# Sums of x on another engine, even token groups and a last expert by eight products, in a fused attention and expert kernel

## The chip, the cores and the metric

The kernel runs on one core of a Trainium2 chip. The metric is the device time of one execution in microseconds; lower is better. A core has TensorE (matrix products, PE in the profile; its weight loads are PEld), VectorE (DVE), ScalarE (ACT), GpSimd (POOL) and SyncE (SP), which issues DMA transfers. Each engine takes its instructions in order and waits for semaphores of the others.

## The reference

Attention with a sketch of degree two gives x; then eight experts are applied to every token, weighted by a routing matrix P.

```python
# attention: B = H = 4, S = 1088, D = 32, r = 8
phi(x) = (S1 x)_i (S2 x)_j                       # 64 features
num = phi(q) @ (phi(k)^T v);  den = phi(q) . sum(phi(k)) + 1e-6
x = (num / den), as (B*S, H*D) = (4352, 128)
# routing: N, D, E, F = 4352, 128, 8, 1024
P = exp(x @ w_gate - max)
for _ in range(8):                               # rows, then columns, are normed
    P /= P.sum(1, keepdims=True) + 1e-9
    P /= P.sum(0, keepdims=True) + 1e-9
    P *= N / E
for e in range(E):
    out += P[:, e:e + 1] * (np.maximum(x @ w1[e], 0) @ w2[e])
```

All is float32.

## The kernel before, in words

**Two ways through an expert.** P is positive, so P * relu(x w1) w2 equals relu((P x) w1) w2. While attention and routing still run, TensorE fills its gaps with experts whose P is not known yet: the *unweighted* stage (`groups`) takes expert 0 for all tokens and expert 1 for tokens 0 to 1279, and keeps the results, transposed, in `kept[0]` and `kept[1]`. They are multiplied by P later, on GpSimd (L933, L935). All other pairs of token and expert are done in the *weighted* stage, the function `weighted()`, after routing.

**Token groups.** An entry of `groups` or `wgroups` is (first token, n, experts); it covers two halves of n tokens each. In the weighted stage `witems` lists (group, expert) pairs, 60 of them; odd groups take their experts in reverse, so that a group often begins with the expert with which the one before ended, whose weights then need no load (`same`). Groups are counted from 0 and so are items. Each item is done in two passes s = 0 and s = 1, for two halves of the hidden dimension; a pass of the first layer (`firsts`) and the second layer's products of the pass before it (`seconds`) are issued in turn, step by step.

**Seven products for eight.** Two blocks by two blocks are multiplied with seven block products and sums of blocks in the manner of Strassen and Winograd. That needs sums of the blocks of w1 (`sum_first`, L864 to L867, into `w1x`), of w2 (`sum_second`, L876 to L879, into `ws`), of x (`sum_x`: part 0 at L902 on GpSimd, parts 1 and 2 at L904 and L906 on VectorE, into `xf`) and of the hidden layer (VectorE, L1058 to L1066, into `ts`, beside the additions L977 and the relus L980). Item 0 uses eight products in the first layer, and group 0 eight in the second. Sums of weights are made once, in group 0, and written to DRAM (L870, L880); later groups load them (L845, L856).

**Where a product's inputs come from.** `weigh(i)` multiplies x by a row of P on GpSimd (L894, into `xf`) and swaps partition halves with two DMAs (L897). `aside`, called once per pass at its third step, puts GpSimd's work there: `weigh` of the item after next and the sums of the next item's weights, each after a one-column copy on ScalarE (`gate`, L989) that holds it back to this point. `spare(0)` and `spare(1)` are places for VectorE at the last two steps of a pass.

**Order of the transfers.** SyncE issues nearly all transfers of this stage in program order: for an item, raw or summed w1 of the next (L850 or L845), the row of P (L886), rows for the kept results (L931), the swaps (L897), the store of w1's sums (L870), w2 of the next (L854), and the store of ws's sums (L880) or their load (L856). A store waits for the sums it writes, and everything behind it waits too.

**End of a group.** Second-layer products accumulate in four PSUM banks `acc[g][rho][q]`. `ended(g, q)` copies them to the tile `z`, of which there is one (L1132, ScalarE). `finish_seven` lists the sums that make the output rows of it: two over z, then a swap of partition halves by DMA into `w` (L1155), nine more sums of 64 rows, and for each half an addition of the kept row (all at L1136), a transpose (L1183) and four stores, one for each head (L676); a store is cut in two at a batch boundary. The list `leisure` is worked off one entry at a time: two in `spare` at s = 0 (VectorE), one in `aside` if it is small and no chore for the kept rows is waiting (GpSimd). What is left at the end is worked off on VectorE.

In the weighted stage all engines keep the program's order (`manual_schedule`). A tile with one buffer may be written for its next use only after the last reader of its former use.

```python
def product(out, form, x, start, stop):
    for r in range(2):
        rows = slice(H2 * r, H2 * (r + 1))
        for col in range(2):
            o = P * s + H2 * col
            nc.tensor.matmul(out[H2 * col:H2 * (col + 1), r], w1[rows, form, o:o + H2], xf[rows, x], ...)
```

Of the kernel before, what the change touches and what calls it, by code (L numbers as in the profile page):

```python
# [10 lines left out]
F32 = mybir.dt.float32  # L11
# [39 lines left out]
def kernel(  # L51
# [477 lines left out]
    def routing():  # L529
# [45 lines left out]
        for b in (1, 0, 2, 3):  # L575
# [20 lines left out]
    kept = [keep.tile([P, N], F32, name="kept0"), keep.tile([P, 1280], F32, name="kept1")]  # L596
    items = [(g, e) for g, group in enumerate(groups) for e in group[2]]
# [301 lines left out]
    def sum_x(i, part_):  # L899
        xf = sources[i]  # L900
        if part_ == 0:
            nc.gpsimd.tensor_tensor(xf[:, 4:6], xf[:, 1:4:2], xf[:, 0:2], op=Alu.subtract)  # L902
# [19 lines left out]
    def chores_of(i):  # L922

        g, e = witems[i]
        lo, n, es = wgroups[g]
        o = [j for j, (h, _) in enumerate(witems) if h == g].index(i) - 1
        ys = [kept[x][:, lo:lo + 2 * n] for x in range(es[0])]
        if not 0 <= o < len(ys):
            return []
        pk = late[0].tile([P, 2 * NW], F32, tag="pk", name="pk", bufs=1)[:, 0:2 * n]  # L930
        nc.sync.dma_start(out=pk, in_=pT[o:o + 1, lo:lo + 2 * n].to_broadcast([P, 2 * n]))  # L931
        halves = [slice(n * t, n * (t + 1)) for t in range(2)]
        chores = [lambda c=c: nc.gpsimd.tensor_tensor(ys[o][:, c], ys[o][:, c], pk[:, c], op=Alu.mult) for c in halves]  # L933
        if o == 1:
            chores += [lambda c=c: nc.gpsimd.tensor_tensor(ys[0][:, c], ys[0][:, c], ys[1][:, c], op=Alu.add)  # L935
                       for c in halves]
        return chores


    def weighted():  # L940
# [16 lines left out]
        def firsts(t):  # L957
# [33 lines left out]
            def aside(y):  # L991


                now = i == 0 or g == 0 and s == 1
# [59 lines left out]
            add(h[:, 3], pc, p1)  # L1054
            if g == 0:
                relu(h[:, 3], h[:, 3])
# [5 lines left out]
            relu(flat(h[:, 1], n), pa)  # L1062
            if g:
                nc.vector.tensor_tensor(ts[:, 2], h[:, 1], ts[:, 0], op=Alu.subtract)  # L1064
# [5 lines left out]
        def seconds(t):  # L1070
# [74 lines left out]
        def finish_seven(g):  # L1145
# [27 lines left out]
            out_of(g, y)  # L1173

        def out_of(g, y):
            lo, n, es = wgroups[g]
            for t in range(2):
                at = lo + n * (1 - t)
                plus(y[:, t], y[:, t], kept[0][:, at:at + n])

                def put(engine, t=t, at=at):
                    yt = late[0].tile([P, NW // 32, 32], F32, tag="yt", name="yt", bufs=2)[:, 0:n // 32, :]
                    nc.vector.transpose(out=yt.rearrange("p b d -> p (b d)"), in_=y[:, t])  # L1183
                    store(yt, at // 32, (at + n) // 32)

                leisure.append((put, False))

# [123 lines left out]
```

## Time and profile before

| | |
|---|---|
| median of 3 runs | 957.92 us (957.33 to 958.08) |
| the profiled execution's own time | 956.46 us |
| its span, first to last instruction | 954.7 us |
| TensorE busy | 907.8 us (95%) |
| VectorE, ScalarE, GpSimd busy | 728.2, 556.8, 253.2 us |
| mean granted TensorE clock | 0.978 |
| read from and written to HBM | 139.33 MB, 19.57 MB |

Durations in the trace belong to the profiled execution. TensorE's products of different array quadrants run at the same time, so the records overlap, and busy is the time in which at least one runs. Idle time of an engine costs nothing unless the chain of waits passes through it. "Idle before" in brackets is the engine's wait ahead of an instruction and what ended it.

### The profile page before, as it was taken

What the parts mean: (1) busy time and instruction counts of PE and PEld (TensorE: products, weight loads), DVE (VectorE), ACT (ScalarE), POOL (GpSimd) and SP (SyncE); (2) the same over time, 40 slices, a digit from 0 to 9 for tenths busy, and PEclk for the clock granted to TensorE, in tenths of its full rate; (3) what the DMA queues carried; (4) which work ended last, traced back from release to release, by engine and by line L of the source; (5) the groups of instructions that cost most, each with busy time, mean ns of one, the idle gap of its engine ahead of it and who ended that gap; (6) DMA issues with size and microseconds to landing.
All of it is one profiled execution on the core that took longest, in us unless ns stands there. A gap on an engine that the chain in (4) does not pass through costs nothing.

```text
span 954.7 us, 35858 instructions
## 1 busy us (share of the span) xinstructions
PE 907.8 (95%) x15452; PEld 635.1 (67%) x15452; DVE 728.2 (76%) x1275; ACT 556.8 (58%) x1116; POOL 253.2 (27%) x298
## 2 busy tenths in 40 slices
PE   9999999988688999999999999999999999999992
PEld 5787544455455667767766776776677778788782
DVE  7688699722222688888888888888888889898894
ACT  3454555554345666666666666666666656666661
POOL 3121100163435222232213323322331232232220
PEclk9999999999879999999999999999999999999996
DMA  9994100456564777468658665856776695684951
GB/s 245 303 272 140 51 1 1 119 188 185 158 178 144 220 224 225 135 194 274 185 164 244 219 184 155 272 184 184 227 240 193 228 290 185 209 281 128 283 200 35
DMA packets 125918, 180.11 MB, mean 189 GB/s; under 512 B 28960, under 2 KB 93552, under 8 KB 118592
## 3 DMA queue, kind: packets, MB, share of 16 engines
q1 hardware_dynamic: 124016, 172.42, 58.9%
q0 software_dynamic: 1600, 5.36, 1.9%
q8 instruction: 122, 2.00, 0.9%
q14 instruction: 36, 0.29, 0.1%
q10 hardware_dynamic: 144, 0.03, 0.0%
HBM read 139.33 MB, written 19.57 MB: 166 GB/s over the span
## 4 chain that ended last, share of the span: by engine, by line
PE 59%; DVE 4%; ACT 2%; issue 2%; POOL 0%; DMA 0%; SPq 0%; ACTq 0%; DVEq 0%; POOLq 0%
PE pair L973 30%; PE s L1092 29%; DVE hb L977 1%; ACT z L1132 1%; DVE hb L1058 1%; DVE hb L1064 1%; DVE z L1136 1%; DVE hb L1065 0%; DVE hb L1066 0%; ACT copies L1036 0%; DMA w<-z 0%; POOL xf L902 0%; DVE y L1136 0%; ACT hb L980 0%; SPq L676 0%
## 5 line engine op out<-in xcount | busy, mean ns | idle before, releaser
L973 PE MATMUL pair<-xf,w1x 64*64 64x256 f32 (+2 forms) x6736 | 516.0, 371 | 27.5 <-POOL xf L902 20.1
L973 PEld LDWEIGHTS pair<-xf,w1x 64*64 64x64 f32 x6736 | 260.9, 134 | 132.9 <-POOL xf L902 23.5
L977 DVE TENSOR_TENSOR hb<-pair,copies 128x512 f32<-128x512 f32 (+2 forms) x354 | 234.1, 664 | 121.4 <-PE pair L973 60.1
L1092 PE MATMUL s<-hb,w 64*64 64x256 f32 (+2 forms) x3440 | 262.6, 374 | 0.2 <-ACT z L1132 0.2
L1092 PE MATMUL s<-hb,ws 64*64 64x256 f32 (+2 forms) x3392 | 255.6, 364 | 0.2 <-DVE hb L1065 0.2
L980 ACT ACTIVATE hb<-hb 128x512 f32<-128x512 f32 (+2 forms) x248 | 151.1, 611 | 119.2 <-DVE hb L977 116.9
L1092 PEld LDWEIGHTS s<-hb,w 64*64 64x64 f32 x3440 | 136.4, 136 | 50.8 <-issue 4.8
L1092 PEld LDWEIGHTS s<-hb,ws 64*64 64x64 f32 x3392 | 135.7, 133 | 42.6 <-DVE hb L1065 0.6
L894 POOL TENSOR_TENSOR xf<-xT,pb 128x512 f32<-128x512 f32 (+2 forms) x60 | 74.7, 1246 | 297.5 <-ACT xf L989 208.3
L902 POOL TENSOR_TENSOR xf<-xf 128x512 f32<-128x512 f32 (+2 forms) x59 | 74.7, 1266 | 192.9 <-ACT xf L989 171.2
L705 PE MATMUL a<-xT,w 128*64 128x416 f32 (+3 forms) x512 | 119.9, 462 | 0.0
L707 ACT ACTIVATE hb<-a 128x416 f32<-128x416 f32 (+3 forms) x128 | 59.3, 466 | 67.3 <-PE a L705 56.4
L1039 ACT COPY copies<-pair 128x512 f32<-128x512 f32 (+2 forms) x118 | 67.0, 568 | 52.8 <-PE pair L973 52.8
L980 ACT ACTIVATE hb<-pair 128x512 f32<-128x512 f32 (+2 forms) x126 | 72.5, 575 | 38.7 <-PE pair L973 38.7
L1042 ACT COPY copies<-pair 128x512 f32<-128x512 f32 (+2 forms) x118 | 66.7, 565 | 37.5 <-PE pair L973 37.5
L1036 ACT COPY copies<-pair 128x512 f32<-128x512 f32 (+2 forms) x118 | 67.0, 568 | 30.5 <-PE pair L973 30.5
L1058 DVE SCALAR_TENSOR_TENSOR hb<-hb 128x512 f32<-128x512 f32 (+2 forms) x106 | 72.2, 681 | 11.4 <-DVE hb L977 0.5
L1064 DVE TENSOR_TENSOR hb<-hb 128x512 f32<-128x512 f32 (+2 forms) x106 | 70.7, 667 | 2.2 <-ACT hb L980 1.1
L720 DVE TENSOR_TENSOR hb<-hb 128x416 f32<-128x416 f32 (+7 forms) x84 | 59.6, 709 | 16.7 <-ACT hb L707 13.4
L766 PE MATMUL s<-hb,ws 128*64 128x416 f32 (+3 forms) x224 | 69.8, 471 | 0.2 <-DVE hb L720 0.2
L1065 DVE SCALAR_TENSOR_TENSOR hb<-hb 128x512 f32<-128x512 f32 (+2 forms) x106 | 69.8, 658 | 0.0
L1066 DVE TENSOR_TENSOR hb<-hb 128x512 f32<-128x512 f32 (+2 forms) x106 | 69.8, 658 | 0.0
(165 smaller groups left out, 649.2 us busy)
## 6 DMA issues: line engine op xcount, KB each, us to landing
w1x<-w1x SPq DMA_DIRECT2D x53, 1024.0 KB, 5.2
w<-in_moe_w_dram SPq DMA_DIRECT2D x57, 512.0 KB, 5.0
ws<-ws SPq DMA_DIRECT2D x53, 512.0 KB, 5.9
pb<-pT SPq DMA_DIRECT2D x42, 256.0 KB, 5.2
xf<-xf SPq DMA_DIRECT2D x84, 128.0 KB, 2.6
w1x<-in_moe_w_dram SPq DMA_DIRECT2D x28, 128.0 KB, 3.9
ph<-qa SPq DMA_DIRECT2D x12, 288.0 KB, 4.7
rb<-qb SPq DMA_DIRECT2D x3, 1152.0 KB
```

Of the source, the lines that this page charges most:

```text
L705: nc.tensor.matmul(ph[sl], loaded_w[j][0][:, P * f + H2 * s:P * f + H2 * (s + 1)], xT[:, at + lo:at + hi], start=True, stop=True, tile_pos ...
L766: nc.tensor.matmul(sums[g][i][H2 * s:H2 * (s + 1)], w, x, start=c == 1, stop=c == per, tile_position=(0, H2 * s))
L894: nc.gpsimd.tensor_tensor(xf[:, 0:2].rearrange("p b n -> p (b n)"), xT[:, lo:lo + 2 * n], weights.pop(i), op=Alu.mult)
L902: nc.gpsimd.tensor_tensor(xf[:, 4:6], xf[:, 1:4:2], xf[:, 0:2], op=Alu.subtract)
L973: nc.tensor.matmul(out[H2 * col:H2 * (col + 1), r], w1[rows, form, o:o + H2], xf[rows, x], start=start, stop=stop, tile_position=(H2 * r, ...
L977: nc.vector.tensor_tensor(flat(out, n), x, flat(y, n), op=Alu.add)
L980: nc.scalar.activation(out=x, in_=y, func=Act.Relu)
L1058: nc.vector.scalar_tensor_tensor(ts[:, 0], h[:, 3], 0.0, h[:, 0], op0=Alu.max, op1=Alu.subtract)
L1064: nc.vector.tensor_tensor(ts[:, 2], h[:, 1], ts[:, 0], op=Alu.subtract)
L1065: nc.vector.scalar_tensor_tensor(ts[:, 1], h[:, 3], 0.0, h[:, 1], op0=Alu.max, op1=Alu.subtract)
L1066: nc.vector.tensor_tensor(ts[:, 3], h[:, 2], ts[:, 2], op=Alu.subtract)
L1092: yield lambda rho=rho, rows=rows, c=c: nc.tensor.matmul(acc[g][rho][q][H2 * half:H2 * (half + 1), n * place:n * (place + 1)], w[rows], fl ...
```

## The change

Three things are changed.

1. In group 0, part 0 of the sum of x is done by VectorE at the last step of the pass before (`spare(1)` at s = 0) and not by GpSimd in `aside` at s = 1; the gate ahead of it goes. The first item of group 1 has it there too.
2. The groups are cut anew. The unweighted stage takes expert 1 up to token 1343 (its last group has n = 416, not 384). The weighted stage has five groups of n = 256 with seven experts, one of 224 with seven, two of 224 with six, one of 224 with five, and a last of 224 with expert 7 alone. Before: six of 256 with seven, two of 224 with six, one of 192 with six. There are still 60 items in the same order of experts.
3. The last group (`LAST`) uses eight products in the second layer, so that the two halves of the tokens end in separate PSUM banks (q = u), the first after the fourth of its eight steps. Its end, `finish_last`, works off `leisure` on VectorE, then adds a half's two accumulators directly to `kept[0]`, transposes it and stores it. Group 8 adds its result into `kept[0]` and no longer stores.

```diff
@@ groups
-              *((1088 + 832 * i, 416, [0]) for i in range(3)), (3584, 384, [0]), (512, 384, [1])]
-    wgroups = [*((1280 + 512 * i, 256, list(range(1, E))) for i in range(6)),
-               (0, 224, list(range(2, E))), (448, 224, list(range(2, E))), (896, 192, list(range(2, E)))]
+              *((1088 + 832 * i, 416, [0]) for i in range(3)), (3584, 384, [0]), (512, 416, [1])]
+    SPLIT = 1344
+    wgroups = [*((SPLIT + 512 * i, 256, list(range(1, E))) for i in range(5)), (3904, 224, list(range(1, E))),
+               *((448 * i, 224, list(range(2, E))) for i in range(2)), (896, 224, list(range(2, E - 1))),
+               (896, 224, [E - 1])]
+    LAST = len(wgroups) - 1
     DIRECT = (0,)
+    whole = (0, LAST)
...
@@ sum_x
-            nc.gpsimd.tensor_tensor(xf[:, 4:6], xf[:, 1:4:2], xf[:, 0:2], op=Alu.subtract)
+            engine = nc.gpsimd if witems[i - 1][0] else nc.vector
+            engine.tensor_tensor(xf[:, 4:6], xf[:, 1:4:2], xf[:, 0:2], op=Alu.subtract)
@@ chores_of
-        ys = [kept[x][:, lo:lo + 2 * n] for x in range(es[0])]
+        ys = [kept[x][:, lo:lo + 2 * n] for x in range(2 if lo < SPLIT else 1)]
+        if g == LAST:
+            return []
@@ aside
-                if s == 1 and i + 1 < len(witems):
+                if s == 1 and i + 1 < len(witems) and g:
                     gate(sources[i + 1][:, 4, 0:1], y)
                     sum_x(i + 1, 0)
@@ spare
                 if s == 1:
                     if i + 1 < len(witems):
                         sum_x(i + 1, 1 + spot)
+                elif g == 0:
+                    if spot:
+                        sum_x(i + 1, 0)
                 else:
                     leave(nc.vector, True)
@@ firsts, item 0
-                        if b == 3 and k and s == 1:
-                            sum_x(1, 1)
-                            sum_x(1, 2)
+                        if b == 3 and k:
+                            for part_ in ((1, 2) if s else (0,)):
+                                sum_x(1, part_)
@@ firsts, last steps
-            if g == 0:
+            if g in whole:
                 relu(h[:, 3], h[:, 3])
...
-            if g:
+            if g not in whole:
                 nc.vector.tensor_tensor(ts[:, 2], h[:, 1], ts[:, 0], op=Alu.subtract)
...
@@ seconds
-                per = 2 * len(es) * (8 if g == 0 else 3 if q else 4)
+                per = 2 * len(es) * (4 if g == LAST else 8 if g == 0 else 3 if q else 4)
...
-            if g == 0:
+            if g in whole:
                 for m, (k, u, b) in enumerate(((0, 0, 0), (1, 0, 2), (0, 1, 3), (1, 1, 1))):
                     for r in range(2):
-                        both(into(0, raw(0, k, r), h[:, b], r, 0, u), into(1, raw(1, k, r), h[:, b], r, 0, u))
-                        if last and m == 3 and r == 1:
+                        q = u if g == LAST else 0
+                        both(into(0, raw(0, k, r), h[:, b], r, q, u), into(1, raw(1, k, r), h[:, b], r, q, u))
+                        if last and m == 3 and r == 1 and g == 0:
                             ended(g, 0)
                             finish_direct(g)
+                        if last and m % 2 and r == 1 and g == LAST:
+                            finish_last(g, u)
@@ out_of
-                plus(y[:, t], y[:, t], kept[0][:, at:at + n])
+                k = kept[0][:, at:at + n]
+                plus(k if g + 1 == LAST else y[:, t], y[:, t], k)
+                if g + 1 < LAST:
+                    leisure.append((lambda engine, t=t, at=at: put(y[:, t], at, n), False))
+
+        def finish_last(g, u):
+            lo, n, es = wgroups[g]
+            while leisure:
+                do = leisure.pop(0)
+                if do:
+                    do[0](nc.vector)
+            at = lo + n * (1 - u)
+            y = kept[0][:, at:at + n]
+            for rho in range(2):
+                nc.vector.tensor_tensor(y, acc[g][rho][u][:, n * u:n * (u + 1)], y, op=Alu.add)
+            put(y, at, n)
```

`put` is the former inner function of `out_of`: the transpose and the stores.

More of the change, by code (lines that the diff above doesn't have):

```diff
@@ L589 @@
     groups = [(0, 256, [0]), (512, 288, [0]), (0, 256, [1]),
-              *((1088 + 832 * i, 416, [0]) for i in range(3)), (3584, 384, [0]), (512, 384, [1])]
-    wgroups = [*((1280 + 512 * i, 256, list(range(1, E))) for i in range(6)),
-               (0, 224, list(range(2, E))), (448, 224, list(range(2, E))), (896, 192, list(range(2, E)))]
+              *((1088 + 832 * i, 416, [0]) for i in range(3)), (3584, 384, [0]), (512, 416, [1])]
[4 more added lines that the diff above has]
+    LAST = len(wgroups) - 1
     DIRECT = (0,)
+    whole = (0, LAST)
     assert sorted((lo, e) for lo, n, es in groups + wgroups for lo in range(lo, lo + 2 * n, 32) for e in es) == [
         (lo, e) for lo in range(0, N, 32) for e in range(E)]
-    kept = [keep.tile([P, N], F32, name="kept0"), keep.tile([P, 1280], F32, name="kept1")]
+    kept = [keep.tile([P, N], F32, name="kept0"), keep.tile([P, SPLIT], F32, name="kept1")]
     items = [(g, e) for g, group in enumerate(groups) for e in group[2]]
@@ L991, in aside @@
             def aside(y):
-                now = i == 0 or g == 0 and s == 1
                 if s == 0 and i + 2 < len(witems):
                     weigh(i + 2, lambda x: gate(x, y))
-                if s == 1 and i + 1 < len(witems):
+                if s == 1 and i + 1 < len(witems) and g:
                     gate(sources[i + 1][:, 4, 0:1], y)
@@ L1173, in finish_seven, with put @@
             out_of(g, y)
+        def put(y, at, n):
+            yt = late[0].tile([P, NW // 32, 32], F32, tag="yt", name="yt", bufs=2)[:, 0:n // 32, :]
+            nc.vector.transpose(out=yt.rearrange("p b d -> p (b d)"), in_=y)
+            store(yt, at // 32, (at + n) // 32)
         def out_of(g, y):
@@ L1178, in out_of @@
                 at = lo + n * (1 - t)
-                plus(y[:, t], y[:, t], kept[0][:, at:at + n])
[L1181 to L1186, printed above, removed]
+                k = kept[0][:, at:at + n]
[13 more added lines that the diff above has]
+            put(y, at, n)
         for t in range(len(todo) + 1):
```

## The prediction

> **What bounds the kernel now.** I read the page first (chain, groups), then the waits, then the busy table cut at the weighted groups, then the timeline of GpSimd, SyncE and TensorE inside group 0, and last the timeline of the end. Groups and experts in the weighted stage are counted from 0, as in the code.
>
> ```profile
> PE 59%; DVE 4%; ACT 2%; issue 2%; POOL 0%; DMA 0%; SPq 0%; ACTq 0%; DVEq 0%; POOLq 0%
> L1064 DVE TENSOR_TENSOR hb<-hb 128x512 f32<-128x512 f32 (+2 forms) x106 | 70.7, 667 | 2.2 <-ACT hb L980 1.1
> ```
>
> The chain is TensorE nearly throughout, so a change counts by the TensorE work it adds, by the stalls of TensorE, and by the tail after the last product. The waits name one stall that the change aims at:
>
> ```profile
> PE pair L973 <- POOL xf L902: 20.1, 7, 4.1
> ```
>
> The cuts below are the starts of the first first-layer product of expert item 1, of group 1, of group 6 (where the width falls to 224), of groups 7 and 8, and the end of the last first-layer product. Columns: length, busy time of PE, PEld, DVE, ACT, POOL, granted clock, DMA share, GB/s.
>
> ```profile
> 203.60:314.10 110.50, 91.99 (x1441) 58.44 (x1444) 30.76 (x50) 52.84 (x106) 47.67 (x58) 0.88 0.57 170
> 314.10:741.93 427.83, 426.11 (x7853) 298.81 (x7848) 363.34 (x605) 273.65 (x509) 113.02 (x98) 1.00 0.67 207
> 741.93:809.24 67.31, 65.12 (x1348) 51.62 (x1344) 57.82 (x106) 43.29 (x89) 20.47 (x21) 1.00 0.76 242
> 809.24:873.72 64.48, 64.18 (x1349) 52.37 (x1345) 57.69 (x108) 43.18 (x89) 20.01 (x22) 1.00 0.72 224
> 873.72:934.34 60.62, 57.77 (x1341) 50.70 (x1336) 53.03 (x107) 38.57 (x85) 15.56 (x19) 1.00 0.62 196
> 934.34:954.70 20.36, 3.01 (x71) 2.17 (x60) 8.51 (x23) 2.21 (x5) 0.00 (x0) 0.63 0.22 41
> ```
>
> Groups 1 to 5 hold 35 items: 12.22 us each. Six items of width 224 took 67.31 us (11.22 each) in group 6 and 64.48 (10.75) in group 7; six of width 192 took 60.62. The six items of group 0 in the first row took 110.50, or 18.4 each, at a mean clock of 0.88, while GpSimd was busy for only 47.67: group 0 waits, but not because GpSimd is full.
>
> What it waits for stands in the timeline (start, duration, engine, line):
>
> ```profile
> 241.19 0.43 SPq L854 DMA_DIRECT2D w<-in_moe_w_dram  x1
> 247.69 0.73 POOL L876 TENSOR_TENSOR ws<-w 128x256 f32<-128x256 f32 x1 [5.68 <-DMA w<-in_moe_w_dram]
> 250.63 0.32 SPq L880 DMA_DIRECT2D ws<-ws  x1
> 251.01 2.53 SPq L850 DMA_DIRECT2D w1x<-in_moe_w_dram  x4
> 257.59 0.72 POOL L864 TENSOR_TENSOR w1x<-w1x 128x256 f32<-128x256 f32 x1 [5.75 <-DMA w1x<-in_moe_w_dram]
> 260.43 1.26 POOL L902 TENSOR_TENSOR xf<-xf 128x512 f32<-128x512 f32 x1
> 260.50 0.33 SPq L870 DMA_DIRECT2D w1x<-w1x  x1
> 260.88 0.43 SPq L854 DMA_DIRECT2D w<-in_moe_w_dram  x1
> 261.75 1.13 PE L973 MATMUL pair<-xf,w1x 64*64 64x256 f32 x8 [3.91 <-POOL xf L902]
> ```
>
> This is a closed ring. SyncE issues in order, and each store of sums stands ahead of the next load. Load of w2 at 241.19, GpSimd's four sums from 247.69, their store at 250.63, the load of the next w1 right behind it at 251.01, four sums from 257.59, their store at 260.50, the next w2 at 260.88: 19.7 us a turn. TensorE and the sum of x (L902) are not links of it; L902 only hangs on its end and holds TensorE until 261.75.
>
> **The change part by part.** *Sum of x on VectorE (group 0).* Seven instructions of 1.26 us leave GpSimd, seven VectorE instructions of about 0.67 us (the 128x512 SBUF row, L1064) come, half an item earlier, and seven ScalarE gate copies go; no DMA moves. VectorE has 30.76 us of work in 110.50 there, so the cost is hidden by its idle time; queued behind each are the three parts of the next hidden layer, which would wait if the swapped halves of x were late, but those are issued an item ahead. TensorE then waits for the four sums of w1 instead, the first of which (L864) ends 3.4 us before L902 did. But the ring keeps its 19.7 us: what an item gains it loses waiting for the next w1. Only the last turn counts. Item 6 can start earlier, and then needs its raw w2 for the second layer:
>
> ```profile
> 299.41 0.42 SPq L854 DMA_DIRECT2D w<-in_moe_w_dram  x1
> w<-in_moe_w_dram SPq DMA_DIRECT2D x1, 512.0 KB, 6.5
> 308.06 0.61 PE L1092 MATMUL s<-hb,w 64*64 64x256 f32 x8
> ```
>
> It lands at 305.9; TensorE used it at 308.06. The gain is at most **-2.1 us**, and I take that; 0 is the other end, if half-speed stretches eat it.
>
> The Trainium skill, SBUF — State Buffer, on the shared port pair, says that a VectorE instruction with two SBUF inputs and a reading GpSimd instruction exclude each other for the whole instruction. By it a moved sum could hold GpSimd up inside the ring; no row here shows the two meeting there, and I leave it out of the sum.
>
> *Token groups.* Expert 1 takes 32 more columns per half in the unweighted stage. There one step of two 64-wide blocks at 384 columns takes 0.65 us:
>
> ```profile
> 181.92 0.81 PE L705 MATMUL a<-xT,w 128*64 128x384 f32 x4
> 182.57 0.81 PE L766 MATMUL s<-hb,w 128*64 128x384 f32 x4
> ```
>
> That is 1.69 ns a column. Four blocks of 4 first-layer steps and 3.5 second-layer ones: 30 x 32 x 1.69 = **+1.6 us**, with TensorE busy all through there.
> Group 5 goes from 256 to 224: by group 7's items 7 x (10.75 - 12.22) = **-10.3**. Groups 6 and 7 stay. Group 8 and the new group 9 together are six items of 224 in place of 192: 64.48 less one step of 0.38, against 60.62: **+3.5**. Only about 1.5 of the 6.8 saved is work (32 columns x 28 steps x 1.69); the rest is stall. At 192 the products alone need 28 x 192 x 1.69 = 9.08 an item, 54.5 in all, so 6.1 us of that row are stalls; group 7 has 0.9, group 6 3.7. I take group 7, whose first expert's weights are already there as in group 8.
>
> *A last group of one expert.* This has a wait that the diff does not show. Group 8 now ends one item earlier. Its accumulators are copied by ScalarE (L1132) into the single tile z in the middle of item 59's first half; but group 7's last two sums that read z are handed to VectorE only behind that half's additions, since group 8 has one item fewer for them to be spread over. ScalarE waits there, with three relus, two copies and the copy of the next half's first product queued behind it; TensorE needs these. Sizes from the same place at the boundary of groups 5 and 6:
>
> ```profile
> 746.20 1.05 ACT L1132 COPY z<-s 128x512 f32<-128x512 f32 x2
> 746.60 0.63 DVE L977 TENSOR_TENSOR hb<-pair,copies 128x448 f32<-128x448 f32 x1 [0.18 <-PE pair L973]
> 747.14 0.59 ACT L980 ACTIVATE hb<-hb 128x448 f32<-128x448 f32 x1
> 748.04 1.08 ACT L1132 COPY z<-s 128x512 f32<-128x512 f32 x2
> 748.98 0.57 ACT L1036 COPY copies<-pair 128x448 f32<-128x448 f32 x1
> 749.61 0.61 PE L973 MATMUL pair<-xf,w1x 64*64 64x224 f32 x8 [0.32 <-ACT copies L1036]
> 932.28 0.39 DVE L1136 TENSOR_TENSOR y<-z 64x224 f32<-64x224 f32 x1
> ```
>
> VectorE is through its last addition at 747.23 and would end two more sums at 748.0; the two copies (1.05), three relus (about 1.65), two copies (1.08) and the copy (0.5) then end at 752.3, not 749.5: 2.7 us later, and 0.3 for one boundary more: **+3.0**. Such a stall can halve the clock:
>
> ```profile
> 236.46:239.88 3.42, 1.91 (x24) 0.76 (x16) 0.00 (x0) 1.18 (x3) 1.90 (x3) 1.00 0.51 158
> 239.88:243.29 3.41, 1.23 (x12) 0.80 (x16) 0.85 (x2) 0.03 (x1) 2.13 (x3) 0.50 0.52 192
> 775.76:779.18 3.42, 1.70 (x36) 0.87 (x29) 1.31 (x3) 1.06 (x2) 2.36 (x3) 1.00 1.11 375
> ```
>
> A stretch of 3.42 us with 24 matmuls was followed by one at 0.50; the one with 36 was not (group 6's row above has 1.00 throughout). A stretch at half clock costs up to 1.7 us, and the new stall of about 2.4 and 0.8 us leaves some 22 to 36 matmuls in a stretch, by where it falls: I add half of 1.4, **+0.7**. The Trainium skill, TensorE: Matmul & The Clock Gate, Part 1, has the clock fall only after a whole idle window of about 3.4 us; by that the term would be 0 and the time 954.5, but the rows show it falling after partly busy ones.
>
> *Eight products in the last item and the tail.* The second layer gains two steps of 0.38 us behind the last first-layer product, hidden by the longer VectorE and DMA chain there:
>
> ```profile
> 936.68 0.40 DVE L1183 STREAM_TRANSPOSE yt<-y 128x224 f32<-128x224 f32 x1
> 937.11 3.76 SPq L676 DMA_DIRECT2D out_dram<-yt  x8
> 940.98 1.29 SPq L1155 DMA_DIRECT2D w<-z  x2
> 944.76 0.35 DVE L1136 TENSOR_TENSOR y<-z,w 64x192 f32<-64x192 f32 x1 [5.73 <-DMA w<-z]
> 947.87 0.36 DVE L1136 TENSOR_TENSOR y<-y,kept 128x192 f32<-128x192 f32 x1
> 948.67 3.71 SPq L676 DMA_DIRECT2D out_dram<-yt  x8
> ```
>
> Counted from the last first-layer product, the tail is 20.4 us. VectorE loses its four subtractions, so the flush of outstanding sums starts at 0.2 instead of 2.3. But it is still all of it: two transposes with eight stores (0.47 each, to 4.4), the swap of halves (3.8 from issue to use, 8.2), nine sums (3.1 at 192, 3.4 at 224), two with the kept rows (0.7, to 12.4). Only then come two additions from PSUM (0.35 to 0.62 each; I take 0.4) and a transpose (13.6), four stores (15.4), and for the second half eight, since tokens 896 to 1119 cross the end of a batch: 19.1. The last issue before ended 2.3 us ahead of the end: 21.4, **+0.9** (0 to +2). The separate banks end the first half early in TensorE's order, but that half waits for the flush anyway.
>
> **Sum.** -2.1 + 1.6 - 10.3 + 3.5 + 3.0 + 0.7 + 0.9 = -2.7 us: span 952.0, profiled execution 953.8 (956.46 now), which stood 1.5 under the median of 957.92; against that, **955.2 us**.
>
> **Rivals.** *The last group's stalls stay* (slower). If the 6.1 us belong to the place and not to the width, because the loads of kept weights and w1 land late, then 5.2 of them come back: 960.4 us. For it: group 6 at 224 is 2.8 us dearer than group 7. Against it: group 7. It decides where a load behind the swap of group 7 lands later than the 10.75 us item allows. Chance 0.20. *GpSimd's queue after all sets group 0's period:* each of five turns 1.26 us shorter, -6.3 instead of -2.1: 951.0; against it 47.67 busy of 110.50, and L902 stands outside the ring. 0.05. *VectorE's sums hold up GpSimd's sums in the ring* by their 0.67 us a turn: +3.4, 958.6; nothing in the rows puts them at the same time. 0.05. *The wait on z does not arise* (the last two sums get out earlier): 951.5; the code speaks against it, 0.13. *All group 0 stalls go*, as the wait table by itself suggests: 20.1 less than now, some 937; the ring speaks against it, 0.03. A gain in group 0 lost to the clock and a longer tail, near 957.5: 0.06.
>
> **How the numbers follow.** The forecast's own case has 0.48, within 953 to 957.5. A measurement of this kernel can tell about 0.2%, 1.9 us, from no change: faster means below 956.0, slower above 959.8. Faster: 0.31 of the forecast's case, 0.13, 0.05, 0.03 = 0.52. Slower: 0.14 of the first rival and 0.03 of held sums with a half-clock stretch more = 0.17. Same: 0.31. The range of 950.5 to 960.6 runs from the case without the wait, 1 us lower, to the first rival.
>
> **What would show it.** Right: stalls on L902 gone from group 0, but stalls on w1's load and L864 to L867 in their place, items 2 to 5 still near 19.7 us; item 7 starting about 2 us earlier after allowing 1.6 for the unweighted stage; an idle ScalarE ahead of L1132 in item 59 and 3 us of TensorE stall behind it; group 8's items near 10.6; a tail of 21. Wrong: a shorter turn of the ring, no wait at L1132, or stalls of over 1 us in group 8.

## The result: slower by half a per cent, and the profile after

| | before | after |
|---|---|---|
| median | 957.92 us (956.63 to 958.08, 5 runs) | 962.38 us (960.71 to 964.97, 5 runs) |
| ratio | | 1.0052, 95% interval 1.0032 to 1.0073 |
| profiled execution, its span | 956.46 us, 954.7 us | 962.38 us, 960.6 us |
| mean granted TensorE clock | 0.978 | 0.985 |

The change made the kernel 4.5 us slower; the prediction had it 2.7 us faster, and the measured time lies 1.8 us above its range. The two traces differ by more, 5.9 us, since the profiled execution of the kernel before is 1.5 us faster than its median and that of the changed kernel is the median. The table of busy times of the changed kernel, cut at the same places as before (columns: length, busy time of PE, PEld, DVE, ACT, POOL, granted clock, DMA share, GB/s), with a first and a fourth row that were not shown of before:

```profile
0.00:193.64 193.64, 191.72 (x1884) 115.45 (x1884) 153.31 (x279) 96.30 (x221) 26.50 (x68) 1.00 0.50 142
206.77:318.59 111.82, 90.94 (x1440) 63.52 (x1444) 33.00 (x54) 52.18 (x100) 39.23 (x52) 0.94 0.53 164
318.59:661.00 342.41, 341.07 (x6285) 241.25 (x6281) 289.39 (x482) 218.79 (x407) 90.50 (x78) 1.00 0.66 205
661.00:738.95 77.95, 75.53 (x1572) 66.45 (x1568) 67.63 (x124) 50.22 (x103) 20.82 (x20) 1.00 0.72 229
738.95:805.67 66.72, 64.89 (x1350) 52.71 (x1348) 57.37 (x106) 43.16 (x89) 19.86 (x21) 1.00 0.79 249
805.67:870.92 65.25, 64.59 (x1348) 55.74 (x1344) 58.36 (x108) 43.12 (x89) 20.88 (x22) 1.00 0.73 224
870.92:938.46 67.54, 65.37 (x1341) 52.31 (x1336) 55.57 (x103) 44.22 (x90) 17.10 (x19) 1.00 0.58 180
938.46:960.60 22.14, 3.96 (x84) 2.91 (x76) 8.27 (x23) 1.04 (x3) 0.00 (x0) 0.66 0.23 43
```

The two rows of the kernel before that answer to the first and the fourth (all before item 0; group 5):

```profile
0.00:190.42 190.42, 188.56 (x1885) 113.99 (x1885) 152.75 (x276) 95.46 (x221) 26.78 (x68) 1.00 0.49 141
656.49:741.93 85.44, 85.07 (x1573) 59.75 (x1568) 73.73 (x124) 54.86 (x103) 22.73 (x20) 1.00 0.70 220
```

| stretch | before | after | difference | forecast |
|---|---|---|---|---|
| up to item 0 | 190.4 | 193.6 | +3.2 | +1.6 |
| items 1 to 6 | 110.5 | 111.8 | +1.3 | -2.1 |
| groups 1 to 4 | 342.4 | 342.4 | 0 | 0 |
| group 5 | 85.4 | 78.0 | -7.5 | -10.3 |
| groups 6 and 7 | 131.8 | 132.0 | +0.2 | 0 |
| group 8 (and 9) | 60.6 | 67.5 | +6.9 | +7.2 |
| tail | 20.4 | 22.1 | +1.8 | +0.9 |
| sum (item 0 stays at 13.1 to 13.2) | | | +5.9 | -2.7 |

Four terms came out worse, by 1.6, 3.4, 2.8 and 0.9 us. Each difference is that of one trace before and one after; where further traces say what of it the change brings, it is told below. The three longest rows of TensorE's waits after show what became of the 20.1 us on the sum of x:

```profile
PE s L1101 <- DMA w<-in_moe_w_dram: 13.6, 5, 3.4
PE pair L980 <- POOL w1x L868: 3.3, 5, 1.7
PE pair L980 <- DMA w1x<-in_moe_w_dram: 2.9, 5, 0.8
```

They are not gone; they stand one step further up, on the landing of w2 and w1 and on GpSimd's first sum of w1: 19.8 us in all.

### The profile page after: what moved, and what is told of

The parts are those of the page before. It is cut to its first block, busy times and chain, and to the rows that moved or that the text cites. A ratio compares the mean times of both kernels' runs of the same rounds, so it can differ in the third digit from the quotient of the medians.

```text
span 960.6 us, 35878 instructions
## 1 busy us (share of the span) xinstructions
PE 909.1 (95%) x15468; PEld 657.4 (68%) x15468; DVE 727.2 (76%) x1278; ACT 556.4 (58%) x1111; POOL 244.6 (25%) x291
## 4 chain that ended last, share of the span: by engine, by line
PE 56%; DVE 4%; ACT 3%; issue 2%; DMA 2%; SPq 1%; POOL 0%; DVEq 0%; ACTq 0%; POOLq 0%
PE pair L980 29%; PE s L1101 28%; ACT z L1144 1%; DVE hb L984 1%; DMA w<-in_moe_w_dram 1%; DVE z L1148 1%; SPq L680 1%; ACT hb L987 1%; DMA ws<-ws 0%; DVE hb L1067 0%; DVE hb L1073 0%; DMA w<-z 0%; DVE hb L1074 0%; ACT copies L1045 0%; DVE hb L1075 0%
## 5 line engine op out<-in xcount | busy, mean ns | idle before, releaser
L980 PE MATMUL pair<-xf,w1x 64*64 64x256 f32 (+1 forms) x6736 | 522.5, 369 | 16.0 <-POOL w1x L868 3.3
L984 DVE TENSOR_TENSOR hb<-pair,copies 128x512 f32<-128x512 f32 (+1 forms) x354 | 233.5, 662 | 161.5 <-PE pair L980 88.6
L1101 PE MATMUL s<-hb,w 64*64 64x256 f32 (+1 forms) x3520 | 272.3, 371 | 15.3 <-DMA w<-in_moe_w_dram 13.6
L1101 PE MATMUL s<-hb,ws 64*64 64x256 f32 (+1 forms) x3328 | 254.6, 364 | 0.0
L987 ACT ACTIVATE hb<-hb 128x512 f32<-128x512 f32 (+1 forms) x250 | 151.8, 609 | 117.6 <-DVE hb L984 113.4
L898 POOL TENSOR_TENSOR xf<-xT,pb 128x512 f32<-128x512 f32 (+1 forms) x60 | 74.7, 1246 | 298.3 <-ACT xf L996 195.8
L907 POOL TENSOR_TENSOR xf<-xf 128x512 f32<-128x512 f32 (+1 forms) x52 | 65.1, 1252 | 188.6 <-ACT xf L996 168.0
L1048 ACT COPY copies<-pair 128x512 f32<-128x512 f32 (+1 forms) x118 | 66.9, 567 | 52.8 <-PE pair L980 52.8
L987 ACT ACTIVATE hb<-pair 128x512 f32<-128x512 f32 (+1 forms) x126 | 72.4, 574 | 37.8 <-PE pair L980 37.7
L1051 ACT COPY copies<-pair 128x512 f32<-128x512 f32 (+1 forms) x118 | 66.6, 564 | 35.7 <-PE pair L980 35.7
L1045 ACT COPY copies<-pair 128x512 f32<-128x512 f32 (+1 forms) x118 | 66.9, 567 | 33.8 <-PE pair L980 33.8
L1067 DVE SCALAR_TENSOR_TENSOR hb<-hb 128x512 f32<-128x512 f32 (+1 forms) x104 | 70.6, 679 | 11.2 <-DVE hb L984 0.5
L724 DVE TENSOR_TENSOR hb<-hb 128x416 f32<-128x416 f32 (+7 forms) x84 | 59.2, 705 | 21.8 <-ACT hb L711 15.7
L1073 DVE TENSOR_TENSOR hb<-hb 128x512 f32<-128x512 f32 (+1 forms) x104 | 68.1, 655 | 2.0 <-ACT hb L987 1.1
L1075 DVE TENSOR_TENSOR hb<-hb 128x512 f32<-128x512 f32 (+1 forms) x104 | 68.9, 662 | 0.0
L1074 DVE SCALAR_TENSOR_TENSOR hb<-hb 128x512 f32<-128x512 f32 (+1 forms) x104 | 68.8, 661 | 0.0
```

The lines of the kernel that those rows point to most:

```text
L898: nc.gpsimd.tensor_tensor(xf[:, 0:2].rearrange("p b n -> p (b n)"), xT[:, lo:lo + 2 * n], weights.pop(i), op=Alu.mult)
L984: nc.vector.tensor_tensor(flat(out, n), x, flat(y, n), op=Alu.add)
L987: nc.scalar.activation(out=x, in_=y, func=Act.Relu)
L1045: nc.scalar.copy(flat(p1, n), pa)
L1067: nc.vector.scalar_tensor_tensor(ts[:, 0], h[:, 3], 0.0, h[:, 0], op0=Alu.max, op1=Alu.subtract)
L1074: nc.vector.scalar_tensor_tensor(ts[:, 1], h[:, 3], 0.0, h[:, 1], op0=Alu.max, op1=Alu.subtract)
```

## The experiments

Lines named in the expectations of a kernel without the group changes are those of the kernel before. Each ratio is against the kernel before, on the same chip.

**One part alone.** The first kernel has only part 1 of the change, the second only the even groups (three groups of 224 with six experts, all by seven products; no last group of one expert), the third both of these, the fourth the whole change with a second tile z:

```diff
 # second and third
+    wgroups = [..., (3904, 224, list(range(1, E))), *((448 * i, 224, list(range(2, E))) for i in range(3))]
 # fourth
-                ends[g] = late[0].tile([P, 2, 2, 2 * NW], F32, tag="z", name="z", bufs=1)
+                ends[g] = late[0].tile([P, 2, 2, 2 * NW], F32, tag="z", name="z", bufs=2)
```

> The kernel before with only the sum of x on VectorE in group 0. Ring theory (loads, GpSimd sums and stores in SyncE's order set group 0's period): items 1 to 6 of the weighted stage take 108 to 113 us as before (110.5), items 2 to 5 each 19 to 20.5, stalls on w1 sums and w1/w2 loads in place of the sum of x; time 955.5 to 959. GpSimd-queue theory: items 1 to 6 take about 104, time 951 to 952. If moving the sum itself makes the loads of w2 land later (6.5 us before, 6.7 to 7.6 in the changed kernel), items 1 to 6 take 111.5 to 113 and the time is 958.5 to 961.

> The kernel before with only the token groups made even: unweighted stage to token 1343, five weighted groups of 256 and one of 224 with seven experts, three of 224 with six. By the changed kernel's items: unweighted stage +2.0, group 5 -7.5, groups 6 and 7 about 0, group 8 +3.3 (six items of 10.6 to 11.1 with a boundary, against 60.6), tail 0: 955.5 to 957. If the stalls of the last group stay at 224 (the rival on record): 960 or more. If the stall of 2.9 us in group 5 of the changed kernel belongs to that one profile: 953.

> The changed kernel without its last group: group 8 has its six experts with seven products each and the old ending. If the last group of one expert costs what the profile says (2.2 us of stall behind the copy of the accumulators, 1.8 us of longer tail, 0 for the products): about 4 us under the changed kernel, 957.5 to 959.5. If the banks ending separately help the tail as the change is put: above the changed kernel, 964 or more.

> The changed kernel with two buffers for the tile z. Theory: ScalarE's copy of group 8's accumulators then waits for no sum of group 7, item 59 takes 10.2 to 10.8 us and not 12.8, the stall of TensorE on that copy and on the relus behind it is gone: 2 us under the changed kernel, 959.5 to 961. Rival (the stall is TensorE's own at a group boundary): no change.

| kernel | median, us | ratio, 95% interval | items 1 to 6 | group 5 | last group(s) | tail |
|---|---|---|---|---|---|---|
| sum of x alone | 957.53 | 1.0005, 0.9991 to 1.0018 | 111.7 | 85.4 | 60.6 | 20.7 |
| even groups alone | 959.86 | 1.0015, 1.0003 to 1.0028 | 112.1 | 77.0 | 64.2 | 22.8 |
| both | 960.82 | 1.0030, 1.0013 to 1.0046 | 113.3 | 78.2 | 65.0 | 23.2 |
| the change with two z | 962.28 | 1.0043, 1.0027 to 1.0060 | 113.3 | 78.5 | 66.4 | 22.2 |

The sum of x on VectorE changes nothing that can be measured. The even groups by themselves lose a little: the trace saves 8.4 us in group 5 and gives back 3.6 at the end, 2.4 in the tail, 1.8 before item 0 and 1.6 in group 0. Both together are 1.6 us below the changed kernel, where about 4 were expected. The second z takes the wait away (item 59, up to the start of its last first-layer product, falls from 12.81 to 11.06 us), but the median falls by only 0.1 us, where about 2 were expected; that the wait costs the whole kernel anything is not shown by the times. So the first expectation held; the other three missed, by 1.3 to 2.9 us above the upper end of the range of the theory.

**Taking the ring apart.** In three kernels the two stores of summed weights are issued from GpSimd's queue, so that no load on SyncE stands behind them: the kernel before, the kernel with part 1 alone, and the changed kernel.

```diff
-        nc.sync.dma_start(out=stores[0], in_=w1)
+        nc.gpsimd.dma_start(out=stores[0], in_=w1)
...
-        nc.sync.dma_start(out=form_stores[witems[i][1]][1], in_=ws)
+        nc.gpsimd.dma_start(out=form_stores[witems[i][1]][1], in_=ws)
```

> The kernel before, but the two stores of summed weights in group 0 (L870, L880) are issued from GpSimd's own queue and not from SyncE's, so that no load stands behind a store that waits. The sum of x stays on GpSimd. Ring theory: the order of stores and loads on SyncE sets group 0's 18.4 us an item; without it items 1 to 6 fall from 110.5 to 80 to 97 us (TensorE's own work is about 13 us an item at full clock) and the time from 957.9 to 928 to 945 us. Rival, that transfers or GpSimd's work set group 0 and the order on SyncE only mirrors it: items 1 to 6 stay at 106 to 113 us and the time within 3 us of 957.9.

> The kernel before with the first part of the change alone (sum of x in group 0 on VectorE) and with the stores of summed weights on GpSimd's queue. Ring theory: with the ring gone the sum of x is on the way to TensorE, so that moving it gains what it could not gain before: items 1 to 6 are 2 to 8 us shorter than in the kernel with the stores moved alone. Rival, that a sum on VectorE by itself lengthens the landing of w2 (41.3 to 42.4 us over six loads against 37.5 and 37.8): 2 to 5 us longer than with the stores moved alone.

> The changed kernel, with the stores of summed weights on GpSimd's queue. Ring theory: the whole of group 0's gain comes here too, 13 to 30 us off 962.4: 932 to 949 us; its difference to the kernel before with the first part and the same stores moved stays what it was without (4.8 us: 962.4 against 957.5), since the groups' terms lie elsewhere. Rival: within 3 us of 962.4.

Measured: 930.87 us (ratio 0.9719, 0.9699 to 0.9739), 924.54 us (0.9657, 0.9641 to 0.9674) and 929.90 us (0.9703, 0.9684 to 0.9723). All three went the way of the ring theory, the last by 2 us more than its range. The busy rows of items 1 to 6, of these three in turn:

```profile
204.31:288.34 84.03, 80.39 (x1441) 52.78 (x1444) 33.17 (x50) 52.96 (x106) 57.90 (x73) 0.96 0.73 240
204.34:282.06 77.72, 77.72 (x1440) 65.63 (x1444) 34.53 (x54) 52.34 (x100) 49.94 (x66) 1.00 0.79 259
206.54:284.26 77.72, 77.72 (x1440) 65.59 (x1444) 36.23 (x54) 52.25 (x100) 50.33 (x66) 1.00 0.79 259
```

With the sum of x on VectorE group 0 is now TensorE's work and nothing else: busy for 77.72 of 77.72 us, 12.95 an item, at full clock. With it on GpSimd 6.3 us remain, all of them in item 1 (19.28 us for 12.97): TensorE's busy time is 2.7 us longer there, at the mean clock of 0.96 in the first of the rows above, and TensorE waits once for the sum, 3.6 us:

```profile
PE pair L973 <- POOL xf L902: 3.6, 1, 3.6
```

So the ring is shown to be the bound of group 0, in the kernel before and after. The move of the sum is worth 6.3 us where the ring is gone, and nothing where it stands. The cost of the other two parts stays: 5.4 us between the last two kernels, 4.8 with the ring.

**Why w2 lands later.** With the ring in place, items 1 to 6 did not get 2.1 us shorter by the move; in the changed kernel's trace they are 1.3 us longer. That 1.3 by itself is within what single traces differ by: the seven with the ring and the sum on VectorE have 109.3 to 113.3 us, the two with it on GpSimd 110.5 and 112.1. The loads of w2 do tell them apart. The links of the ring, from the issue on SyncE to GpSimd's first sum, added up over the turns:

| kernel | six loads of w2 | five loads of w1 | first load of w2 to last sum |
|---|---|---|---|
| before | 37.5 | 30.8 | 101.4 |
| even groups alone | 37.8 | 32.1 | 103.0 |
| changed | 41.8 | 29.7 | 104.6 |
| sum of x alone | 42.3 | 29.2 | 104.7 |

The same turn after as shown of before, from the timelines of SyncE and GpSimd:

```profile
245.43 0.43 SPq L858 DMA_DIRECT2D w<-in_moe_w_dram  x1
252.74 0.72 POOL L880 TENSOR_TENSOR ws<-w 128x256 f32<-128x256 f32 x1 [7.71 <-DMA w<-in_moe_w_dram]
255.65 0.32 SPq L884 DMA_DIRECT2D ws<-ws  x1
256.02 3.22 SPq L854 DMA_DIRECT2D w1x<-in_moe_w_dram  x4
```

From the load of w2 to the first sum are 7.31 us, where 6.50 stood. Over the six loads the seven traces with the ring and the sum on VectorE have 39.0 to 42.4 us (39.0 in that with the moved z sum, below, whose group 0 is the changed kernel's). Two kernels with part 1 alone ask why: one lets GpSimd make the sum of x a second time on TensorE's path, the other lets GpSimd make it into a tile that nobody reads.

```diff
 # first
+                        nc.gpsimd.tensor_tensor(again[:, 4:6], again[:, 1:4:2], again[:, 0:2], op=Alu.subtract)
 # second
+                    nc.gpsimd.tensor_tensor(other..., again[:, 1:4:2], again[:, 0:2], op=Alu.subtract)
```

> The first part of the change alone, but GpSimd makes the same sum of x once more in its old place in group 0 (the values are the same), so that TensorE starts an item as late as in the kernel before while VectorE's added instructions are there too. The ring is left as it was. If w2's loads land later because TensorE, ScalarE and VectorE then work beside the store and the load from their start: the six loads of w2 to GpSimd's first sum add up to 37 to 38.5 us as in the kernel before. If VectorE's added instructions do it: 41 to 42.5 us. Time within 2 us of 957.9 by both.

> The first part of the change alone (sum of x on VectorE), and in GpSimd's old place the same sum once more into a tile that nobody reads, so that GpSimd is as busy as in the kernel before while TensorE needs not wait for it. If w2's loads landed later because TensorE, VectorE and ScalarE run from the start of the store and the load: the six loads of w2 to GpSimd's first sum stay at 41 to 42.5 us. If GpSimd's 1.26 us beside the start of the store is what made them shorter in the kernel before: 37 to 38.5 us.

The first: 37.6 us over the six loads; 959.62 us, ratio 1.0032 (1.0015 to 1.0048). So VectorE's added instructions don't do it. The second: 40.1 us, and a single execution of 954.98 us. That lies between the two expectations, and within the 39.0 to 42.4 of the kernels with the sum moved: the third and fourth load took 7.65 and 7.34 us, as in most of them, the fifth 6.48, as before (6.49 in the trace with 39.0). What is shown is that the longer landing comes with an item that TensorE starts earlier: no trace in which it does has less than 39.0, none of the three in which it does not has more than 37.8. That GpSimd's work shortens it at all is not shown. By which resource TensorE, ScalarE and VectorE delay the load stays open.

**The tail.** From the start of the changed kernel's last end on, every second store of output rows goes to ScalarE's queue.

```diff
-                nc.sync.dma_start(
+                (nc.scalar if rear[0] and r % 2 else nc.sync).dma_start(
```

> The changed kernel, but from the start of its last end on every second store of output rows is issued from ScalarE's queue and not from SyncE's. Theory that issue on one queue carries the tail: the eight stores ahead of the swap of halves and the twelve at the end take half as long to issue (4.53 to 2.3 us and 5.60 to 2.8 us), the tail falls from 22.1 to 17 to 18.5 us and the time from 962.4 to 957.5 to 959 us. Rival, that the landing of the transfers carries it: the tail stays at 21.5 to 22.5 us, 961.5 to 963 us.

958.94 us, ratio 1.0017 (1.0002 to 1.0032); the tail is 17.9 us. The timelines of SyncE at the end, first of the changed kernel, then of this one:

```profile
938.92 4.53 SPq L680 DMA_DIRECT2D out_dram<-yt  x8
943.56 1.29 SPq L1167 DMA_DIRECT2D w<-z  x2
953.09 5.60 SPq L680 DMA_DIRECT2D out_dram<-yt  x12
```

```profile
939.83 2.65 SPq L682 DMA_DIRECT2D out_dram<-yt  x4
942.58 1.30 SPq L1169 DMA_DIRECT2D w<-z  x2
952.11 2.96 SPq L682 DMA_DIRECT2D out_dram<-yt  x6
```

Issue on one queue carried the tail, as expected: counted from the last first-layer product, the last issue starts its run 14.6 us on in the first kernel and 12.7 in the second, and lasts half as long.

**Group 5.** At the end of group 4, VectorE's second sum over z is put one place later in the list:

```diff
                 plus(z[:, 0, q, 0:2 * n], z[:, 0, q, 0:2 * n], z[:, 1, q, 0:2 * n])
+                if g == 4 and q == 0:
+                    leisure.append(None)
```

> The changed kernel; at the end of group 4 VectorE's second sum over z (L1148) is put one place later in the list of leisure sums, so that it doesn't start beside GpSimd's sum of x for the next item (L907). Theory that the two exclude each other, so that VectorE's sum takes 1.65 us in place of 0.68 and TensorE waits 1.3 us behind it: the sum takes 0.68 or 1.15 us, item 36 falls from 12.16 to 11.2 us, group 5 from 78.0 to 77.0 or less. Rival, that TensorE waits there for the boundary's copies or for transfers: item 36 stays at 12.1 to 12.2 us.

The timeline of the changed kernel in item 36 is the reason for it:

```profile
680.84 1.14 POOL L907 TENSOR_TENSOR xf<-xf 128x448 f32<-128x448 f32 x1 [0.90 <-ACT xf L996]
680.87 1.65 DVE L1148 TENSOR_TENSOR z<-z 128x512 f32<-128x512 f32 x1
682.44 1.14 DVE L984 TENSOR_TENSOR hb<-pair,copies 128x448 f32<-128x448 f32 x2
683.11 0.61 PE L980 MATMUL pair<-xf,w1x 64*64 64x224 f32 x8 [1.34 <-DVE hb L984]
```

VectorE's sum started 0.03 us after GpSimd's and took 1.65 us; moved by one place it takes its usual time (timeline of VectorE in that kernel), and group 5 is 2.7 us shorter (its busy row; the second row is groups 8 and 9):

```profile
686.04 0.69 DVE L1148 TENSOR_TENSOR z<-z 128x512 f32<-128x512 f32 x1
658.25:733.47 75.22, 74.90 (x1573) 59.49 (x1569) 66.53 (x122) 50.25 (x103) 22.36 (x22) 1.00 0.76 240
865.78:937.78 72.00, 67.94 (x1340) 52.83 (x1336) 55.18 (x103) 44.09 (x90) 16.60 (x19) 0.95 0.55 169
```

Item 36 falls from 12.16 to 10.59 us, items 38 and 39 from 22.50 to 21.33. The first is the moved sum's. The second need not be: items 38 and 39 have 21.2 to 23.05 us over the traces with this width, and 21.19 in two whose sum over z was as slow as in the changed kernel. Of the nine traces of kernels with the width of 224 in group 5, the six in which that sum has 1.64 or 1.65 us have an item 36 of 12.15 or 12.16, with the ring or without; the others have 11.19, 11.19 and 10.59 with sums of 1.15, 1.15 and 0.69. The whole execution, 962.19 us, shows no gain, and there is only this one: groups 8 and 9 had 72.0 us there, with stretches at half clock in items 57 and 59 (14.73 and 14.34 us for 11.19 and 12.81).

**What the parts add up to.** Three kernels with the stores on GpSimd's queue, put together from the edits above: part 1 with the old groups and two queues at the end; the whole change with two z and two queues; the even groups and part 1 without the last group.

> The kernel before with the first part of the change (sum of x on VectorE in group 0), the stores of summed weights on GpSimd's queue, and at the end every second store of output rows on ScalarE's queue; the token groups of before. If the three terms add (924.5 us for the first two, 3.4 us measured for the two queues at the end of the changed kernel, here eight and eight stores): 920.5 to 922.5 us, the tail 17 from 20.5. If the last transfers' landing carries this tail: 924 to 925.5.

> The changed kernel whole, with the stores of summed weights on GpSimd's queue, two tiles z, and two queues at the end. If the terms add (929.9 less 3.4 for the queues, less 0 to 1.7 for the second z): 924.5 to 926.5 us, which is still 3 to 5 us above the old groups with the same two remedies: the new groups then cost in the unweighted stage, the 224 columns of the last items and the tail, and not in the wait for z. If the wait for z was the whole of their cost: within 1 us of the old groups.

> The changed kernel without the last group of one expert (three groups of 224 with six experts, all by seven products), stores of summed weights on GpSimd's queue. Theory: the even groups by themselves gain in group 5 (7 to 8.5 us) what they lose in the unweighted stage (2), at the width of 224 in place of 192 (4) and in the tail (2.5), and the last group adds 1.5 to 3 us of its own: 924 to 927 us, between the old groups (924.5) and the changed kernel (929.9). Rival, that the even groups cost all of the 5.4 us: 929 to 931.

Measured: 921.62 us (ratio 0.9625, 0.9609 to 0.9640), 923.48 us (0.9642, 0.9619 to 0.9666) and 926.00 us (0.9674, 0.9657 to 0.9691). The first is the fastest kernel of this study, 36 us below the kernel before and 41 below the changed one. The second gained 6.4 us by the second z and the two queues where 3.4 to 5.1 were expected; it is 1.9 us above the first, outside both expectations, and their intervals overlap: no gain of the new groups is shown. Not all of their stalls are mended there: item 36 still has 12.16 us in that trace, with VectorE's sum over z at 1.64. Moving that sum too was not run; by the 1.57 us of item 36 above, an estimate, it would bring the new groups about level with the old. The third lies where it was expected, 3.9 us below the changed kernel with the ring broken; that makes the last group's price 3.9 us there, more than the 1.5 to 3 it was put at.

## Why the prediction was wrong, point by point

**Group 0 (-2.1, came out +1.3).** The reading was right: the ring sets the period, the sum of x is not a link, the wait moves to w2 and to the first sum of w1, and only the last turn could gain. In the changed kernel item 6's first product starts at 300.37 and its second layer waits for w2, issued at 305.78, until 312.53. The step that failed is that "the ring keeps its 19.7 us". It became 3.2 us longer over its length (101.4 to 104.6), by the later landing of w2; -2.1 and 3.2 make 1.1 of the 1.3. The amount is that of one trace (the same group 0 had 103.1 in the one with the moved z sum), but none of the seven has items 1 to 6 as much as 2.1 below the 110.5 of before. The term should have had an upper end above 0: a step outside a ring that starts earlier can still meet the ring's transfers.

**Before item 0 (+1.6, came out +3.2).** TensorE's busy time there rose by as much (188.56 to 191.72). Of the 3.2, 1.17 us lie ahead of all that was changed: the first product of the unweighted stage starts at 18.21 in the trace before and at 19.53 after, and at 17.9 to 19.5 over all sixteen traces. From the first product of 384 columns, in the last group that is still the same, to item 0 it is 45.48 us before (45.4 to 45.6 in the seven traces with the old groups) and 47.53 after, so the change's part is 2.05. The forecast's step was sized right: with the even groups alone the stretch has 46.99 us, 1.5 more. What the prediction put at nothing is the moved sum of x. In the eight traces that have it together with the even groups the stretch has 47.5 to 48.1 us. There VectorE makes item 1's three sums of x (L907, L909, L911) between the last sums of the unweighted hidden layer (L724), which TensorE's last second-layer products read. The first rows are of the changed kernel, the last is of the even groups alone, where nothing stands between these sums (timelines of VectorE):

```profile
188.38 1.02 DVE L724 TENSOR_TENSOR hb<-hb 128x832 f32<-128x832 f32 x1 [1.12 <-PE s L770]
189.32 0.68 DVE L907 TENSOR_TENSOR xf<-xf 128x512 f32<-128x512 f32 x1
189.93 0.58 DVE L724 TENSOR_TENSOR hb<-hb 128x416 f32<-128x416 f32 x1
190.43 0.42 DVE L909 TENSOR_TENSOR xf<-xf 128x256 f32<-128x256 f32 x1
190.76 0.58 DVE L724 TENSOR_TENSOR hb<-hb 128x416 f32<-128x416 f32 x1
```

```profile
187.51 2.28 DVE L721 TENSOR_TENSOR hb<-hb 128x832 f32<-128x832 f32 x3 [1.13 <-PE s L767]
```

In five of the eight traces TensorE's waits name that sum of VectorE, with 0.2 to 0.7 us; with the even groups alone none does. With the old groups the move costs nothing there. No run was made for this, and the even groups alone have one trace.

**Group 5 (-10.3, came out -7.5).** The step that failed is the row taken for the width of 224: group 7's 10.75 us an item. Group 5 begins, as group 6 did, behind a group of 256, and had 11.14, near group 6's 11.22. The prediction saw that row and put its surplus down to group 6 alone. The experiment with the moved z sum shows what 1.6 of the 2.8 us were: item 36, where VectorE's sum over z started beside GpSimd's sum of x. That group 5 then had 75.2 us, the forecast's 75.25, is partly luck: the other 1.2 us lie in items 38 and 39, and what sets those stays open. The Trainium skill, SBUF — State Buffer, section on SBUF's two separate sides, says that a VectorE instruction with two SBUF inputs and a GpSimd instruction that reads SBUF lock each other out of a shared port pair for the whole instruction; the trace agrees, with 1.65 us in place of 0.68. In the trace before, at the same place, VectorE's sum started 0.03 us ahead of GpSimd's and kept its 0.68; there GpSimd's took 1.78 us, in place of the 1.26 of the row in group 0. VectorE's additions L984, with one input in PSUM, overlapped GpSimd's sums and kept their 0.69 us (0.62 at the width of 224). The prediction named this rule, and looked for it only in group 0.

**Groups 8 and 9 (+7.2, came out +6.9).** The wait for z is where it was said to be. ScalarE waits for VectorE's last two sums, and TensorE for ScalarE (timelines of VectorE, ScalarE and TensorE in item 59):

```profile
930.55 0.69 DVE L1148 TENSOR_TENSOR y<-z 64x224 f32<-64x224 f32 x2
931.32 0.97 ACT L1144 COPY z<-s 128x448 f32<-128x448 f32 x2 [1.63 <-DVE y L1148]
933.72 0.61 PE L980 MATMUL pair<-xf,w1x 64*64 64x224 f32 x8 [0.78 <-ACT hb L987]
935.01 0.61 PE L980 MATMUL pair<-xf,w1x 64*64 64x224 f32 x8 [0.30 <-ACT copies L1045]
```

Its size was 1.75 us (item 59 with one z and with two) where 2.7 was forecast. That the sum agrees to 0.3 us is partly luck: the half clock, counted at 0.7, did not come in this trace (it did in that of the moved z sum), while items 54 to 58 took 54.6 us, 0.8 more than five at 10.75, and item 59 without the wait 11.06 us, 0.7 more than one at 10.75 less a step of 0.38, of which 0.3 were forecast for the boundary. The prediction's remark that 1.5 of the 6.8 us saved at 192 are work is a slip: 1.5 us is one item's work, and six items make 9.1; no term rests on it. In the trace with the moved z sum, the busy rows of item 57 show such a stretch and the one before it:

```profile
898.59:902.00 3.41, 1.29 (x28) 0.56 (x20) 0.86 (x2) 0.69 (x2) 2.35 (x3) 1.00 1.15 326
902.00:905.41 3.41, 3.41 (x40) 2.57 (x40) 2.50 (x5) 1.09 (x3) 1.33 (x2) 0.50 0.65 262
```

TensorE waited there 2.1 us for a sum of x, was busy for 1.29 of 3.41 us, and then had half the clock. By the Trainium skill, TensorE: Matmul & The Clock Gate, Part 1, a whole idle window of about 3.4 us comes ahead of that; these rows differ from it, as those of the prediction did.

**The tail (+0.9, came out +1.8).** Its order was right and its size too small; the eight stores took 0.57 us each and not 0.47, and the swap 4.2 us from issue to use and not 3.8. The term stayed within its bounds of 0 to +2.

**The rivals.** The first, 5.2 us of stalls in group 8, gave a time near the measured one by a cause that is not there: items 54 to 58 stay at 10.59 to 11.19 us. GpSimd's queue is not the bound while the ring stands, but behind it, 6.3 us in item 1. VectorE's sums did not hold up GpSimd's in the changed kernel (0.72 to 0.74 us each; one of 0.96 and one of 1.06 have their like before, 0.93 and 1.03). Where they met, in the kernel that makes the sum twice, they did, by 0.45 us:

```profile
251.89 0.73 DVE L903 TENSOR_TENSOR xf<-xf 128x512 f32<-128x512 f32 x1
252.03 1.18 POOL L879 TENSOR_TENSOR ws<-w,ws 128x256 f32<-128x256 f32 x1
```

The range was too narrow on its upper side because group 0 and group 5 each stood in it at their best value, and the moved sum's cost before item 0 at nothing.

## What to carry to other kernels

When a wait's releaser hangs on the end of a closed chain of transfers, ask which link keeps the next transfer from being issued, and move that: here two stores on another queue gave 27 to 35 us, and the engine's work that the wait table named gave nothing before them and 6.3 us after. A moved instruction can be in the way at its new place, even where its engine is idle on the average of the stretch. When a group of instructions gets a new width, take its time from a group with the same neighbours, and read its boundary items apart from the rest. In tail code count the issues on one queue: a last piece that crosses a batch boundary costs four more, and a second queue halves them.

## What the runs showed of the hardware

VectorE's sum of two SBUF tiles beside a GpSimd sum took up to 1.65 us in place of 0.68, and GpSimd's 1.18 in place of 0.73 where VectorE was first. A store issued from GpSimd's queue took 0.57 to 0.60 us of GpSimd's time, and the stores landed later there than from SyncE (w1's sums: median 6.2 to 6.8 us for 5.0 to 5.6); neither was on the path. A load of w2 landed up to 1.8 us later (8.31 us to GpSimd's sum, in the kernel with part 1 alone, for 6.53) where TensorE's products started ahead of it.
